# Turning the last batch's queries and keys on TensorE instead of in transposing DMAs

## Chip, cores and metric

The kernel runs on one core of a Trainium2 chip. The metric is device time in microseconds (us); lower is better. Engines are called as the profile calls them: PE (TensorE; PEld is its weight load), DVE (VectorE), ACT (ScalarE), POOL (GpSimd), SP (SyncE, which here only issues transfers).

## What is computed

Chunked attention over q, k, v of shape (4 batches, 8 heads, 768 rows, 64), and on its result x (4, 768, 512) a Fourier mixing and an MLP:

```python
for c in range(nc):                       # chunks of 32 rows
    k_full = concat([mem_k, k[c_start-16 : c_end+8]])    # clipped at the ends; v alike
    a = softmax(q_c @ k_full.T / sqrt(D))
    out[c] = a @ v_full
x = out.transpose(0, 2, 1, 3).reshape(B, S, H * D)
u = x + real(fft(fft(x, axis=1), axis=2))
un = (u - mean(u)) / sqrt(var(u) + 1e-6)
out = u + relu(un @ w_ch1) @ w_ch2
```

## The kernel before

**Stages.** The four batches go through three stages each: attention for 4 pairs of heads (two heads share the 128 partitions), Fourier mixing, MLP. A pair is numbered n = 0 to 15; batch b has the pairs 4b to 4b+3.

*Attention of a pair* (`attention(n)`). POOL loads q and k in bf16 into qs and ks (three buffers each), 8 rows of a head side by side in one partition. Both must be turned, so that the 64 head dimensions lie on the partitions. SP loads v into va (four buffers). PE forms the scores sc of 64 queries against 128 keys in two halves g (`e_scores`, L433 is its matmul), ACT takes the exponential e (L440), PE forms the weighted values xa (L456) and DVE divides by the sums into xsb (L466, L467).

*Two ways of turning.* Batches below `TURNED` (3 before, so batches 0 to 2) turn on PE: `e_turn_q` and `e_turn_k` issue 16 transposes each (L374) into a PSUM tile trq or trk, and ACT copies them to qT (`e_qT`, L391) and to kTb (`e_kT`, L415). From batch 1 on trq and trk share one PSUM bank, "tr". Batch 3 turns by DMA: its loads come as two transfers each, one per head, in pieces of 64 elements (L343; the other batches have one transfer in pieces of 512, L347), then SP issues one transposing transfer for q into qT (`e_flip_q`, L379) and one for k into kU (`e_flip_k`, L382), and ACT copies kU to kTb (L410). The eight rows of a partition then stand apart in qT, so the scores of batch 3 read q and write sc in strides (L430, L431). Two memsets of kU at the start (L851) go with this way.

*Fourier mixing* (`fourier(b)`): folds on DVE and ACT (zy, pq, ff, hi, lo), matmuls with cosine and sine tables into ps (L528, for the first batch L668), split again into up, matmuls over the columns into pm (L679, L579), sums into xsb on DVE. For batches 1 to 3 the lower half of the attention's result goes out to DRAM and comes back in reversed row order: x_rows on POOL (L562), x_back on SP (L566, L567), xr on POOL (L571); it is added at L586 and L588. Statistics (L693) and un on ACT (L699) follow, and for batches 1 to 3 SP turns un into unT by transposing transfers (`e_flip`, L711).

*MLP* (`mlp(b)`): in two halves of 384 rows, 16 groups ph of 4 matmuls (L741), each with a relu on ACT into hT (L749), then 3 groups pc of 16 matmuls (L756), each with a sum on DVE into osb (L763) and a transfer out (L768, or through DRAM for the reversed rows, L771 and L778).

**The order.** Nothing of it is left to a runtime scheduler: class `Plan` simulates the engines ahead of time, with the cost of each task, the transfers' shares and landings (`late` adds to a landing), counts of free buffers (`take` and `give`) and due times, and each engine's instructions are issued in the order that this gives. PE's MLP tasks have the lowest priority and fill the time in which no attention or mixing task of a later batch is ready. `behind` keeps a task from being issued ahead of another: the loads of pair 12 were behind batch 1's xr (`t_xr[b - 2]`) because pair 12 is `TURNED * HP`; other loads are behind the load of the pair before. On the chip each engine works through its own list in order and waits at semaphores.

Of the kernel before, what the change touches and what calls it, by code (L numbers as in the profile page):

```python
# [177 lines left out]
def kernel(  # L178
# [58 lines left out]
    ks = [spool.tile([KP, 2, RB * D], BF16, name=f"ks{i}") for i in range(NS)]  # L237
# [4 lines left out]
    kU = [spool.tile([P, RB, KS], BF16, name=f"kU{i}") for i in range(NKU)]  # L242
    kTb = [spool.tile([P, NT, P], BF16, name=f"kTb{i}") for i in range(NKT)]

    TURNED = 3
    cp_q = "p h j d -> p h (j d)"
    HP = H // 2
    seq = [(b, pr) for b in range(B) for pr in (0, 2, 1, 3)]
# [89 lines left out]
    def e_load_qk(n, i):  # L338
        b, pr = seq[n]
        src, dst = ((q, qs), (k, ks))[i]  # L340
        if b >= TURNED:
            for hh in range(2):
# [65 lines left out]
    def e_kT(n, eng=None):  # L408
        if n >= TURNED * HP:
            nc.scalar.copy(  # L410
# [10 lines left out]
    def e_scores(n, g):  # L421
        qT, kT = qT_of[n], kTb[n % NKT]
        sc_of[n, g] = sc = aps.tile([P, 2, 8, 64], FP32, tag="sc", bufs=1, name="sc")
        for t6 in range(6):
            t = 6 * g + t6
            for hh in range(2):
                r0 = 64 * hh
                if n < TURNED * HP:
                    own, to = qT[r0:r0 + 64, ts(t, 64)], sc[:, hh, t6, :]
                else:  # L430
                    own = strided(qT[r0:r0 + 64], t * 64 // RB, [[QP, RB], [1, 64 // RB]])  # L431
                    to = strided(sc[:, hh, t6, :], 0, [[1, RB], [RB, 64 // RB]])
                nc.tensor.matmul(to, kT[r0:r0 + 64, t, :], own, start=True, stop=True,  # L433
                                 tile_position=(r0, 0))
# [415 lines left out]
    t_gate, LATE, t_flip = None, 1.0, [None]  # L850
    t_uz = add("POOL", 0.4, lambda: [nc.gpsimd.memset(kU[i], 0.0) for i in range(NKU)], rank=20)  # L851

    def attention(n):
        nonlocal t_gate
        b, pr = seq[n]
        first = b == 0
        lq, lk = [add("POOL", 1.6 if b >= TURNED else 0.9, lambda i=i: e_load_qk(n, i),
                      take=(("qs", "ks")[i],), moved=3.1 if b >= TURNED else 1.2, grain=0.032 if b >= TURNED else 0.1, late=LATE if b else 0.0,
                      behind=t_gate if n == HP else t_xr[b - 2] if n == TURNED * HP else t_ck.get(n - 1),
                      rank={0: -4 + i, 1: -1.2 + 0.1 * i, 2: 10 + 0.1 * i}.get(n)) for i in range(2)]  # L860
        lv = add("SP", 2.5, lambda: e_load_v(n), [t_ones[n] if n < NV else None],
                 behind=t_x2.get(b - 2),
                 take=("va",), moved=2.6, grain=0.031, head=0.4, late=(0.0, 4.0, LATE, LATE)[b])
        t_lv[n] = lv
        t_ck[n] = lk
        if n == HP - 1:
            def e_gate():
                nc.gpsimd.tensor_copy(gate[64:65], va[n % NV][64:65, 1, NT - 1, 0:1])

            t_gate = add("POOL", 0.1, e_gate, [lv])  # L870
        mk = t_mk[n] = add("DVE", 0.2, lambda: e_mkT(n), [t_mkT, t_kTz[n % NKT], t_mk.get(n - 1)],
                           take=("kTb",))
        if b >= TURNED:
            eq = add("SP", 1.2, lambda: e_flip_q(n), [lq], take=("qT",), give=("qs",),
                     late=5.0, loose=True, behind=t_flip[0])
            t_flip[0] = tk = add("SP", 1.2, lambda: e_flip_k(n), [lk, t_uz], take=("kU",),
                                 give=("ks",), late=5.0, loose=True, behind=eq)
            ek = add("ACT", 2.05, lambda: e_kT(n), [tk, mk], give=("kU",))
        else:
            tq = add("PE", 0.40, lambda: e_turn_q(n), [lq, t_idb], take=("tr",), give=("qs",))  # L880
            dve = ("DVE", nc.vector.tensor_copy) if n < HP else ("ACT", None)
            eq = add("ACT", 0.80, lambda: e_qT(n), [tq], take=("qT",), give=("tr",),
                     rank=SINES - 0.5 if n == 0 else None)
            ktag = "acc" if first else "tr"
            tk = add("PE", 0.43, lambda: e_turn_k(n), [lk, t_idb, t_kz if n == 0 else t_kzs],
                     take=(ktag,), give=("ks",))
            ek = add(dve[0], 1.25 if dve[1] else 1.04, lambda: e_kT(n, dve[1]), [tk, mk],
                     give=(ktag,))
        for g in range(2):
            s_ = add("PE", 0.32, lambda g=g: e_scores(n, g), [eq, ek], take=("sc",),  # L890
                     give=("qT", "kTb") if g == 1 else ())
            t_sc[n, g] = s_
            t_exp[n, g] = x_ = add("ACT", 1.12, lambda g=g: e_exp(n, g),
                     [s_, t_masks, t_after.get(n)], take=("e1",), give=("sc",))
            tag = "mlp" if first and g == 1 else "xa"
            v_ = add("PE", 0.85, lambda g=g: e_values(n, g), [x_, lv, t_low[n % NV]], take=(tag,),
                     rank=len(plan.tasks) + (50 if (n, g) == (2, 1) else 25) if first else None,
                     give=("e1", "va") if g == 1 else ("e1",))
            take = ("xsb",) if g == 0 and n % HP == 0 else ()
            t_norm[n, g] = add("DVE", 0.78, lambda g=g: e_norm(n, g),  # L900
                               [v_, t_norm[n - n % HP, 0] if (n % HP, g) != (0, 0) else None],
                               take=take,
                               give=(tag,))
        return x_
# [142 lines left out]
    def columns_of(b, t_rest):  # L1047
        t_dn, t_un, cols = {}, {}, {}
        allr = list(t_rest.values())
        kts, sa = (0, 1, 2, 3, 4, 5), None  # L1050
        if b == 0:
            for par in range(2):
                for ab in range(2):
                    t_dn[par, ab] = add("DVE", 0.36, lambda par=par, ab=ab: e_dn(b, par, ab),
                                        [t_rest[par, ab]],
                                        take=("dn",) if (par, ab) == (0, 0) else ())
        else:
            kts = (0, 1, 3, 4, 2, 5)

        def columns(kt):  # L1060
            if b > 0 and kt > 2:
                if kt == 3:
                    cols[kt] = add("PE", 0.7, lambda: e_last_row(b), [t_sum[0]])
                return
            give = (("up",) * 4 if kt == 2 else ("dn",) if kt == 5 else ())
            cols[kt] = add("PE", 0.9, lambda: e_columns(b, kt),
                           allr + [t_rows] + (list(t_dn.values()) if kt > 2 else []),
                           take=("acc",), rank=len(plan.tasks) + (15 if kt == 3 else 0),
                           give=give)

        t_sum = {}
        columns(kts[0])
        for i, kt in enumerate(kts):
            if i + 1 < NST and not (b > 0 and kts[i + 1] == 3):
                columns(kts[i + 1])
            if b == 0 or kt < 3:
                su = add("DVE", 0.7, lambda kt=kt: e_sum(b, kt), [cols[kt]],
                         give=("acc",) if b == 0 else ())
                t_sum[kt] = su
                if b > 0 and kt == 0:  # L1080
                    columns(3)
            else:
                su = add("DVE", 0.8, lambda kt=kt: e_sum_back(b, kt - 3),
                         [cols.get(kt), t_sum[kt - 3], t_xr[b]],
                         give=("acc", "dn") if kt == 5 else ("acc",))
            sa = add("DVE", 0.9, lambda kt=kt: e_stats(b, kt), [su, sa])
            un = add("ACT", 0.72, lambda kt=kt: e_un(b, kt), [sa], take=("un",))
            if b > 0:
                t_un[kt] = add("SP", 1.2, lambda kt=kt: e_flip(b, kt),
                               [un], behind=t_un.get(kts[i - 1]) if i else None,  # L1090
                               take=("unT",) if i == 0 else (), give=("un",), late=2.5,
                               loose=True)
                continue
            tp = add("PE", 0.26, lambda kt=kt: e_turn_u(b, kt), [un, t_idh], take=("mlp",),
                     give=("un",))
            t_un[kt] = add("DVE", 0.43, lambda kt=kt: e_unT(b, kt), [tp, t_un.get(kt - 1)],
                           take=("unT",) if kt == 0 else (), give=("mlp",))
        rs = add("POOL", 1.0, lambda: e_rstd(b), [sa])
        return t_un, rs
# [89 lines left out]
```

## Time and profile before

| | us |
|---|---|
| median of 3 runs (lowest, highest) | 291.2 (290.92, 291.56) |
| the profiled execution | 290.92 |
| its span, first to last instruction | 289.2 |
| PE busy in it | 272.9 (94%) |
| ACT, DVE, POOL busy | 167.7, 166.0, 65.1 |
| mean granted clock of PE | 0.999 |

How to read it: a group of instructions has its line, engine, operation, out<-in with the shape, the count, then busy us and mean ns of one, then the idle time just before them with what ended it. The mean of a PE matmul is the time from its start to its modelled end; matmuls overlap, so a block of several is read from the chain of work or from start to start. In the chain, each piece has its start, its length and what it was. The table of stretches has the busy time of each engine between two times.

### The profile page before, as it was taken

What the parts mean: (1) busy time and instruction counts of PE and PEld (TensorE: products, weight loads), DVE (VectorE), ACT (ScalarE), POOL (GpSimd) and SP (SyncE); (2) the same over time, 40 slices, a digit from 0 to 9 for tenths busy, and PEclk for the clock granted to TensorE, in tenths of its full rate; (3) what the DMA queues carried; (4) which work ended last, traced back from release to release, by engine and by line L of the source; (5) the groups of instructions that cost most, each with busy time, mean ns of one, the idle gap of its engine ahead of it and who ended that gap; (6) DMA issues with size and microseconds to landing.
All of it is one profiled execution on the core that took longest, in us unless ns stands there. A gap on an engine that the chain in (4) does not pass through costs nothing.

```text
span 289.2 us, 7127 instructions
## 1 busy us (share of the span) xinstructions
PE 272.9 (94%) x2932; PEld 170.5 (59%) x2932; DVE 166.0 (57%) x345; ACT 167.7 (58%) x290; POOL 65.1 (23%) x115
## 2 busy tenths in 40 slices
PE   1588989999999999999999999999999999999994
PEld 1466678866665767556676656556654544645641
DVE  7967998862239876958675984985672012012011
ACT  6887446688777587836796466526660721712700
POOL 8844893330210172441001002010020000000000
PEclk9999999999999999999999999999999999999999
DMA  6998989999999999999797047784142504004204
GB/s 110 198 174 150 199 159 206 199 201 195 198 190 257 130 223 166 138 152 220 177 173 176 27 111 145 175 141 159 20 89 85 100 9 125 14 36 105 42 36 109
DMA packets 115968, 39.92 MB, mean 138 GB/s; under 512 B 104544, under 2 KB 111200, under 8 KB 115936
## 3 DMA queue, kind: packets, MB, share of 16 engines
q1 hardware_dynamic: 93744, 23.41, 44.8%
q0 software_dynamic: 21472, 15.21, 32.5%
q10 hardware_dynamic: 720, 0.85, 0.9%
q8 instruction: 23, 0.38, 0.5%
q14 instruction: 9, 0.07, 0.1%
HBM read 37.36 MB, written 13.37 MB: 175 GB/s over the span
## 4 chain that ended last, share of the span: by engine, by line
PE 85%; DVE 6%; POOL 5%; DMA 2%; issue 2%; ACT 0%; POOLq 0%
PE pc L756 29%; PE ph L741 29%; PE xa L456 7%; PE ps L528 5%; PE pm L679 5%; PE sc L433 3%; DMA ks<-in_k_dram 2%; PE trk L374 1%; DVE ff L615 1%; PE trq L374 1%; POOL qs L347 1%; DVE hl L635 1%; DVE up L545 1%; DVE xsb L467 1%; PE pm L579 1%
## 5 line engine op out<-in xcount | busy, mean ns | idle before, releaser
L749 ACT ACTIVATE hT<-ph 128x384 f16<-128x384 f32 x128 | 61.9, 491 | 50.6 <-PE ph L741 49.8
L741 PE MATMUL ph<-unT,w_sb 128*128 128x384 f16 x512 | 88.1, 326 | 0.0
L756 PE MATMUL pc<-w_sb,hT 128*128 128x512 f16 x384 | 87.8, 380 | 0.0
L741 PEld LDWEIGHTS <-w_sb 128*128 128x128 f16 x512 | 48.6, 98 | 32.0 <-issue 0.4
L756 PEld LDWEIGHTS <-hT 128*128 128x128 f16 x384 | 35.9, 98 | 41.0 <-issue 0.4
L763 DVE SCALAR_TENSOR_TENSOR osb<-pc,rstd,xsb 128x512 f32<-128x512 f32 x24 | 18.0, 751 | 69.3 <-PE pc L756 64.8
L440 ACT ACTIVATE e<-sc,mbias 128x384 f32<-128x384 f32 x64 | 33.6, 577 | 18.8 <-PE sc L433 18.8
L456 PEld LDWEIGHTS xa<-va,e 128*64 128x64 f32 x672 | 21.9, 137 | 7.2 <-issue 6.2
L456 PE MATMUL xa<-va,e 128*64 128x65 f32 x672 | 25.8, 226 | 0.0
L699 ACT ACTIVATE un<-xsb,mu_s 128x512 f16<-128x512 f32 x24 | 16.9, 719 | 6.6 <-DVE mu_s L694 6.6
L540 ACT CAST up<-ps 128x386 f16<-128x386 f32 x16 | 9.6, 602 | 13.8 <-PE ps L528 11.6
L693 DVE BATCH_NORM_STATS2 st<-xsb 128x6 f32<-128x512 f32 x24 | 16.6, 691 | 0.7
L467 DVE TENSOR_TENSOR xsb<-xa,zs 128x384 f32<-128x384 f32 x28 | 15.6, 558 | 1.0
L466 DVE RECIPROCAL zs<-xa 128x6 f32<-128x6 f32 x28 | 5.3, 190 | 18.1 <-PE xa L456 17.7
L518 DVE TENSOR_TENSOR lo<-ff,hi 128x768 f16<-128x768 f32 x12 | 11.4, 954 | 4.7 <-ACT hi L513 4.7
L545 DVE TENSOR_TENSOR up<-ps,up 128x386 f16<-128x386 f32 x16 | 9.5, 596 | 6.9 <-ACT up L540 6.7
L433 PE MATMUL sc<-qT,kTb 64*128 64x64 bf16 x384 | 12.6, 205 | 0.5 <-ACT e L440 0.5
L433 PEld LDWEIGHTS <-kTb 64*128 64x128 bf16 x384 | 8.5, 100 | 7.3 <-issue 6.1
L571 POOL DMA_DIRECT2D xr<-x_back x3 | 2.3, 778 | 44.3 <-DMA x_back<-x_rows 44.3
L513 ACT CAST hi<-ff 128x768 f16<-128x768 f32 x12 | 9.9, 827 | 3.3 <-DVE ff L505 3.0
L374 PE MATMUL trq<-ident_b,qs 96*64 96x96 bf16 x192 | 7.0, 220 | 5.1 <-DMA qs<-in_q_dram 5.1
L685 DVE TENSOR_TENSOR xsb<-pm,xsb 128x512 f32<-128x512 f32 x15 | 10.0, 672 | 3.2 <-PE pm L679 3.2
(150 smaller groups left out, 356.9 us busy)
## 6 DMA issues: line engine op xcount, KB each, us to landing
va<-in_v_dram SPq DMA_DIRECT2D x32, 220.0 KB
w_sb<-in_moe_w_ch_dram POOLq DMA_DIRECT2D x8, 512.0 KB, 15.1
out_dram<-osb SPq DMA_DIRECT2D x12, 256.0 KB
qs<-in_q_dram POOLq DMA_DIRECT2D x12, 192.0 KB, 6.2
ks<-in_k_dram POOLq DMA_DIRECT2D x12, 192.0 KB, 6.9
x_rows<-xsb POOLq DMA_DIRECT2D x3, 768.0 KB, 5.1
xr<-x_back POOLq DMA_DIRECT2D x3, 768.0 KB, 6.5
out_rows<-osb SPq DMA_DIRECT2D x9, 256.0 KB
```

Source lines behind the costliest of these rows:

```text
L433: nc.tensor.matmul(to, kT[r0:r0 + 64, t, :], own, start=True, stop=True, tile_position=(r0, 0))
L440: nc.scalar.activation(e1[:, :, :, ts(half, 32)], sc[:, :, 0:6, ts(half, 32)], AFT.Exp, bias=mbias[:, half:half + 1], scale=1.0 / math.sqr ...
L456: nc.tensor.matmul(xa[64 * half:64 * half + 64, st, hh, 0:65], e1[:, hh, t6, :], v1[:, hh, 6 * g + t6, 0:65], start=True, stop=True)
L467: nc.vector.tensor_tensor(xs[b][:, 3 * g:3 * g + 3, 2 * pr * D:(2 * pr + 2) * D] .rearrange("p s (h d) -> p s h d", h=2), xa[:, :, :, 0:D] ...
L528: nc.tensor.matmul(out_[:, sp, :], part[:, ab, sp * 3 + st, c0:c1], tab[:, sp, st, :], start=(st == 0 and i == 0), stop=(st == 2 and i == 1))
L679: nc.tensor.matmul(pm[:, par, :], lhs, rhs[:, par, :], start=(im == 0), stop=(im == 3))
L693: nc.vector.bn_stats(st6, xs[b][:, kt, :])
L699: nc.scalar.activation(un, xs[b][:, kt, :], AFT.Identity, bias=mu_of[b][:, kt, 0:1], scale=-1.0)
L741: nc.tensor.matmul(ph[:, 0:384], w1_sb[:, dt, ts(ht, P)], unT_of[b][:, dt, sh * 384:(sh + 1) * 384], start=(dt == 0), stop=(dt == NDT - 1))
L749: nc.scalar.activation(hT_of[b, sh][:, ht, :], ph[:, 0:384], AFT.Relu, bias=0.0, scale=-1.0)
L756: nc.tensor.matmul(pc_of[b, sh, stl], hT_of[b, sh][:, ht, ts(stl, P)], w2_sb[:, ht, :], start=(ht == 0), stop=(ht == NHT - 1))
L763: nc.vector.scalar_tensor_tensor(osb, pc, rstd_of[b][:, st:st + 1], xs[b][:, st, :], ALU.mult, ALU.add)
```

## The change

`TURNED` goes from 3 to 9. There are four batches, so every batch now turns q and k on PE: for pairs 12 to 15 the plan adds the two turns on PE, and the copy of q on ACT reads PSUM; the 8 transposing transfers and the 16 loads by head fall away, 8 loads of the common kind take their place, and the copy of k reads trk instead of kU. The hold of pair 12's loads behind batch 1's xr no longer applies (no pair is number 36), so they come behind pair 11's. The memsets of kU stay in the program.

In `e_scores` two lines are ordered differently, with the same meaning. In the plan, the time that a transposing transfer is given to land after its issue goes from 5.0 to 1.6 for q and k (no longer reached) and from 2.5 to 1.6 for unT.

```diff
-    TURNED = 3
+    TURNED = 9
...
-                if n < TURNED * HP:
-                    own, to = qT[r0:r0 + 64, ts(t, 64)], sc[:, hh, t6, :]
-                else:
+                own, to = qT[r0:r0 + 64, ts(t, 64)], sc[:, hh, t6, :]
+                if n >= TURNED * HP:
                     own = strided(qT[r0:r0 + 64], t * 64 // RB, [[QP, RB], [1, 64 // RB]])
                     to = strided(sc[:, hh, t6, :], 0, [[1, RB], [RB, 64 // RB]])
...
             eq = add("SP", 1.2, lambda: e_flip_q(n), [lq], take=("qT",), give=("qs",),
-                     late=5.0, loose=True, behind=t_flip[0])
+                     late=1.6, loose=True, behind=t_flip[0])
             t_flip[0] = tk = add("SP", 1.2, lambda: e_flip_k(n), [lk, t_uz], take=("kU",),
-                                 give=("ks",), late=5.0, loose=True, behind=eq)
+                                 give=("ks",), late=1.6, loose=True, behind=eq)
...
                 t_un[kt] = add("SP", 1.2, lambda kt=kt: e_flip(b, kt),
                                [un], behind=t_un.get(kts[i - 1]) if i else None,
-                               take=("unT",) if i == 0 else (), give=("un",), late=2.5,
+                               take=("unT",) if i == 0 else (), give=("un",), late=1.6,
                                loose=True)
```

The changed kernel has one line less from L428 on: L433 becomes L432, L741 becomes L740 and so on.

## Prediction

> **What bounds the kernel now.** I read the page's slices first, then the busy time by stretch, then the chain of work that ended last.
>
> ```profile
> PE   1588989999999999999999999999999999999994
> ...
> PEclk9999999999999999999999999999999999999999
> ...
> PE 85%; DVE 6%; POOL 5%; DMA 2%; issue 2%; ACT 0%; POOLq 0%
> ```
>
> From the seventh slice on PE is busy nine tenths or more, at the full granted clock, and 85% of the chain lies on it. A digit 9 may still hide small gaps, so I asked for the busy time of each engine in five stretches (columns: stretch, its length, then PE, PEld, DVE, ACT, POOL busy, clock, DMA share, GB/s):
>
> ```profile
> 47.00:118.60 71.60, 71.48 (x1048) 48.14 (x1046) 46.95 (x98) 53.00 (x93) 19.49 (x28) 1.00 1.24 192
> 118.60:170.60 52.00, 52.00 (x583) 32.14 (x583) 37.64 (x76) 35.03 (x56) 6.65 (x9) 1.00 0.94 153
> 170.60:212.60 42.00, 42.00 (x316) 26.32 (x315) 30.83 (x56) 23.83 (x45) 3.20 (x4) 1.00 0.57 123
> 212.60:285.20 72.60, 72.60 (x384) 37.37 (x382) 9.87 (x16) 25.47 (x52) 1.59 (x2) 1.00 0.28 68
> ```
>
> PE is busy 238.08 of the 238.2 us from 47.0 to 285.2, and the view of waits for that stretch names none on PE. MLP matmuls of earlier batches fill every hole that attention and mixing leave. So from 47 us on the kernel's time is the sum of PE's work; what other engines and queues do counts only if it makes PE wait. The last 4.0 us (285.2 to 289.2) are the last osb and its transfer, and 1.7 us lie outside the span (290.92 against 289.2).
>
> The order of instructions of both programs tells where they part. On PE they are the same up to 118.6 us of this trace; ACT, DVE and SP part at about the same place, POOL at 80 us. The start is therefore the same, with its two memsets of kU, which stay although nothing reads kU any more. The last 64 ph and 48 pc matmuls, the osb and the transfer are the same too. The price is made between 118.6 and 212.6 us.
>
> **Part 1: PE's added and removed work.** The prices are in the chain, in order of time (columns: start, us, what):
>
> ```profile
> 110.12 0.46 PE trq L374 x16
> ...
> 115.71 0.47 PE trk L374 x16
> ...
> 118.68 0.28 PE sc L433 x12
> ...
> 131.71 0.44 PE sc L433 x12
> ...
> 274.85 10.37 PE pc L756 x48
> 285.25 0.75 DVE osb L763
> ```
>
> Added: batch 3 has 4 head pairs, and each now gets a trq block and a trk block of 16 transposes. They cost 0.46 and 0.47 us where PE is saturated, so 4 x (0.46 + 0.47) = 3.72 us. I take the blocks, not the mean of 220 ns of one transpose: that is latency, and the starts lie some 29 ns apart. Removed: the scores of batch 3 read q in strides and write in strides. Their 8 blocks (131.7 to 168 us) take 0.44 us each, while those of batches 1 and 2 take 0.28; the batch now has the short form. That is 8 x 0.16 = 1.28 us back. Nothing else on PE changes in number: 512 ph, 384 pc, 301 ps, 138 pm, 384 sc and 768 value matmuls stand in both programs. A change from a small tile (sc, xa, trq, trk) to a large one costs about 0.1 us (eight pc take 1.83 us ahead of a small tile and 1.73 ahead of a large one); there are 47 such changes before and 47 after, so I add nothing for them. Sum: 3.72 - 1.28 = +2.44 us, all on the path, since PE has no gap to put it in.
>
> One rule speaks much louder against the change. The trace's row is 0.46 us for 16 transposes at a granted clock of 1.00. The Trainium skill ("TensorE: Matmul & The Clock Gate", Part 4: PE-mode transpose) has about 275 ns for one bf16 transpose within a kernel, because the access latency dominates, and says that transposes don't count as busy for the clock gate. By 275 ns, 128 transposes would cost 35.2 us and the kernel would end at about 325 us; by the row it is 3.72 us, and the measured blocks decide.
>
> **Part 2: the other engines.** The four rows that change on ACT:
>
> ```profile
> L391 ACT COPY qT<-trq 128x768 bf16<-128x768 bf16 x12 | 9.6, 797 | 3.0 <-PE trq L374 3.0
> ...
> L415 ACT COPY kTb<-trk 128x1056 bf16<-128x1056 bf16 x8 | 8.3, 1038 | 0.6 <-PE trk L374 0.6
> L410 ACT COPY kTb<-kU 128x1056 bf16<-128x1056 bf16 x4 | 8.2, 2059 | 1.5 <-DMA kU<-ks 1.5
> ```
>
> ACT gains 4 qT copies of 0.80 and its 4 kTb copies go from 2.06 to 1.04: 3.2 - 4.1 = -0.9 us, on an engine that is busy 59 of the 94 us. No gain in time: PE did not wait for it.
>
> POOL issues 8 loads at 0.64 us in place of 16 at 0.77 us (5.1 against 12.3). The loads of pair 12 now go ahead of batch 1's x_rows, those of pair 13 ahead of its xr. Pair 12's k load needs trk of pair 9, done at 86.1 us; x_rows was issued at 86.56 and now goes at about 86.8, with 192 KB ahead of it. Its x_back and xr follow; xr was issued at 100.31, lands some 6.5 us later and is first read at 116.37, so nearly 10 us cover it. rstd of batch 1 now stands behind pair 15's k load (issued at about 122.9) and runs at 123.6, against 123.75 before.
>
> SP loses 8 transposes of some 1.25 us, which stood between the v loads, the six unT transposes of batch 1 and x_back of batch 2. All of those go earlier or stay. PE waited for none of them, so I count nothing.
>
> **Part 3: the shorter landing in the plan** (1.6 for 2.5 us) only moves unT's use in PE's order. Batch 3's unT transposes were issued from 207.5 to 216.3 us and their first reader stands at 243.7; batch 2's were done at 177.7, with their reader at 197.7. Nothing, with 20 us and more of cover.
>
> **Part 4: new waits.** What before does not show is how PE waits in the new order. Below zero it can't go, since PE waits nowhere after 47 us. From above I walked the new PE order with the block times of the chain, from 118.9 us: trq and trk of pair 12 stand at 118.9 and 122.4, of 13 at 126.7 and 129.3, of 14 at 132.6 and 134.1, of 15 at 136.7 and 148.2. Two things can be late.
>
> The loads: those of pair 14 are issued at 110.5 and 116.1, of 15 at 119.4 and 122.9 (each needs the buffer that the transposes of three pairs earlier leave). The same instruction before:
>
> ```profile
> DMA to landing us min/median/max: 4.1/6.5/19.0
> ```
>
> With 6.5 us the least cover (119.4 to 136.7, 17.3 us) leaves 10.8; with the worst, 19.0, q of pair 15 comes 1.7 us late. The strided loads in this very stretch landed in at most 8.9, so I take zero and keep 1.7.
>
> The one tr bank: trq, its copy to qT, trk, its copy to kTb, and the next trq wait for each other. By ACT's order trk of pair 14 comes 0.3 us after qT's copy ends, trq of pair 15 0.4 us after kTb's, the others 0.7 us and more. If one pair of exps (1.05 us) came ahead of the copy at both tight spots, PE would lose 2 x 1.05 - 0.7 = 1.4 us. The same ring served batches 1 and 2 with no wait of PE after 47 us, so I take zero and keep 1.4.
>
> **Sum.** 290.92 + 2.44 = 293.4 us against the profiled execution. The median of the runs lies 0.28 above that execution; I forecast 293.5.
>
> **Rivals.** *PE waits in the new order*: both prices of part 4, up to +3.1 more, so 294 to 296.6. For it: margins of 0.3 and 0.4 us, and a denser attention stage (four pairs between 119 and 164). Against it: no wait in the same pattern of batches 1 and 2. 10%.
>
> *Not slower, by transposes that fit beside matmuls*: if their weight loads and drains overlapped with the neighbours, a block would cost less than it shows. The point from which this decides is 1.28 / 8 = 0.16 us a block; at 0.13 the time would be 290.92 + 1.04 - 1.28 = 290.7. Against it: the blocks' 0.46 is already from start to start between neighbours, with no gap. 6%.
>
> *Removed transfers were slowing PE*: the 8 transposes and 768-packet loads gone, DMA's share falls (0.94 in the stretch 118.6 to 170.6). But 48 pc take 10.36 us with DMA idle or busy, and 20 take 4.42 in both 121 and 192 us. It would give about 292, hardly less. 4%.
>
> **Numbers.** My forecast, with waits under 0.5 us in sum: 80% (293.0 to 294.1). What a measurement can tell from no change is about 0.2%, 0.6 us. The first rival is slower as well, the third mostly; the second splits between same and faster. So slower 0.91, same 0.05, faster 0.04. The range reaches a little into the third case and over half of the first: 292.6 to 295.2.
>
> **What would show it.** Right: trq and trk blocks of 0.46 and 0.47 between 118 and 150 us, sc blocks of 0.28 throughout, PE busy about 275.3 us (272.9 + 2.44), still no waits of PE after 47 us, the last pc at about 287.7. Wrong: waits of PE on ACT's qT or kTb copy, or on ks or qs; transpose blocks much off 0.46; or a start before 118 us that is not the same.

## The result and the profile after

The changed kernel took 293.76 us (median of 5 runs, 293.64 to 294.54) against 291.13 us of the kernel before (5 runs): ratio 1.0094, 95% interval 1.0078 to 1.0109. It is slower, by 2.6 us or 0.9%. The profiled execution took 293.64 us, with a span of 291.9.

The slices of the page and the chain's shares, of the changed kernel:

```profile
PE   1588989999999999999999999999999999999994
...
PEclk9999999999999999999999999999999999999999
...
PE 86%; POOL 5%; DVE 4%; DMA 2%; issue 1%; POOLq 0%
```

The stretches (columns as before; the last two borders lie later, since the program is longer):

```profile
47.00:118.60 71.60, 71.60 (x1060) 48.42 (x1061) 46.90 (x98) 53.11 (x93) 14.91 (x22) 1.00 1.09 194
118.60:170.60 52.00, 52.00 (x703) 33.49 (x702) 38.88 (x79) 35.53 (x61) 4.50 (x6) 1.00 0.61 118
170.60:215.00 44.40, 44.40 (x328) 27.28 (x325) 31.50 (x58) 23.56 (x46) 4.80 (x6) 1.00 0.59 129
215.00:287.80 72.80, 72.80 (x385) 37.45 (x383) 8.26 (x11) 24.33 (x50) 0.00 (x0) 1.00 0.26 64
```

PE is busy in every microsecond from 47.0 to 287.8, 275.1 us in all for 272.9 before, and waits for nothing. DMA's share between 118.6 and 170.6 fell from 0.94 to 0.61 and the time rose: the queues were not the bound.

The chain of the changed kernel where the new blocks stand:

```profile
119.28 0.46 PE trq L374 x16
...
122.83 0.47 PE trk L374 x16
...
132.96 0.46 PE trq L374 x16
133.42 0.71 PE xa L455 x24
134.13 0.28 PE sc L432 x12
134.41 0.49 PE trk L374 x16
...
137.02 0.46 PE trq L374 x16
...
148.38 0.36 PE trk L374 x16
...
277.44 10.37 PE pc L755 x48
287.84 0.75 DVE osb L762
```

Seven of the eight blocks (two of them left out here) cost 0.46 to 0.49 us, the last 0.36; the scores cost 0.28.

**A ruler for the rest.** The start of the kernel, which is the same in nearly all of these programs, drifts by up to 1.3 us from one profiled execution to the next, as its first loads land (the chain of work has 5.32 us for one k load before and 6.11 for the same load after). So I measure from the first transpose of pair 9's k, at about 86 us, to the start of the last 48 pc matmuls, which every kernel with at least ten pairs turned on PE has in common: PE works without a gap between them unless it waits. The first of these transposes, before and after, on the timeline:

```profile
85.64 0.55 PE L374 MATMUL trk<-turn_b,ks 100*64 100x100 bf16 x16
```

```profile
85.96 0.55 PE L374 MATMUL trk<-turn_b,ks 100*64 100x100 bf16 x16
```

Before: 85.64 to 274.85, 189.21 us. After: 85.96 to 277.44, 191.48 us. The change cost PE 2.27 us; 0.32 of the two profiled executions' difference is the start.

### The profile page after: what moved, and what is told of

It is laid out like the page before. It is cut to its first block, busy times and chain, and to the rows that moved or that the text cites. A ratio compares the mean times of both kernels' runs of the same rounds, so it can differ in the third digit from the quotient of the medians.

```text
span 291.9 us, 7361 instructions
## 1 busy us (share of the span) xinstructions
PE 275.1 (94%) x3060; PEld 172.8 (59%) x3060; DVE 166.8 (57%) x345; ACT 166.5 (57%) x294; POOL 57.6 (20%) x107
## 4 chain that ended last, share of the span: by engine, by line
PE 86%; POOL 5%; DVE 4%; DMA 2%; issue 1%; POOLq 0%
PE ph L740 29%; PE pc L755 29%; PE xa L455 7%; PE ps L527 5%; PE pm L678 5%; PE sc L432 3%; DMA ks<-in_k_dram 2%; PE trk L374 2%; PE ps L667 2%; PE trq L374 2%; DVE ff L614 1%; POOL qs L347 1%; DVE hl L634 1%; DVE xsb L466 1%; PE pm L578 1%
## 5 line engine op out<-in xcount | busy, mean ns | idle before, releaser
L740 PE MATMUL ph<-unT,w_sb 128*128 128x384 f16 x512 | 87.9, 326 | 0.0
L740 PEld LDWEIGHTS <-w_sb 128*128 128x128 f16 x512 | 48.6, 98 | 32.4 <-issue 0.6
L391 ACT COPY qT<-trq 128x768 bf16<-128x768 bf16 x16 | 12.7, 797 | 4.9 <-PE trq L374 4.9
L347 POOL DMA_DIRECT2D qs<-in_q_dram x16 | 10.5, 658 | 24.1 <-PE trq L374 14.9
L374 PE MATMUL trq<-ident_b,qs 96*64 96x96 bf16 x256 | 9.1, 218 | 6.4 <-DMA qs<-in_q_dram 6.4
L347 POOL DMA_DIRECT2D ks<-in_k_dram x16 | 10.3, 644 | 23.3 <-PE trk L374 22.8
L415 ACT COPY kTb<-trk 128x1056 bf16<-128x1056 bf16 x12 | 12.5, 1040 | 0.7 <-PE trk L374 0.6
```

The lines of the kernel that those rows point to most:

```text
L347: nc.gpsimd.dma_start(dst[n % NS][0:QP], src[b, 2 * pr:2 * pr + 2].rearrange("h (p j) d -> p h (j d)", j=RB))
L374: nc.tensor.transpose(out_[64 * hh:64 * hh + 64, j * w:(j + 1) * w], src[:, hh, j * D:(j + 1) * D], eye)
L740: nc.tensor.matmul(ph[:, 0:384], w1_sb[:, dt, ts(ht, P)], unT_of[b][:, dt, sh * 384:(sh + 1) * 384], start=(dt == 0), stop=(dt == NDT - 1))
```

## Experiments

"Ruler" is that length in the profiled execution; the times are medians, compared with runs of the kernel before on the same chip.

| kernel | median us | before | ratio (95%) | ruler us |
|---|---|---|---|---|
| after | 293.76 | 291.13 | 1.0094 (1.0078, 1.0109) | 191.48 |
| shorter landings only | 292.62 | 291.36 | 1.0038 (1.0018, 1.0058) | 190.74 |
| batch 3 turned twice | 296.58 | 291.36 | 1.0170 (1.0141, 1.0199) | 194.26 |
| strided scores kept | 294.76 | 291.36 | 1.0105 (1.0076, 1.0134) | 192.74 |
| batches 2, 3 by DMA | 330.12 | 291.36 | 1.1318 (1.1272, 1.1364) | - |
| the same, pair 12 held | 317.93 | 290.96 | 1.0937 (1.0914, 1.0960) | - |
| pairs 14, 15 by DMA | 292.65 | 290.96 | 1.0056 (1.0043, 1.0068) | 190.39 |
| pairs 10 to 15 by DMA | 296.52 | 290.96 | 1.0153 (1.0120, 1.0187) | 197.00 |
| after without kU memsets | 293.80 | 290.96 | 1.0104 (1.0084, 1.0125) | 191.48 |
| pairs 10 to 15, x_back first | 294.71 | 291.35 | 1.0088 (1.0055, 1.0120) | 189.88 |
| pairs 11 to 15, x_back first | 290.74 | 291.35 | 0.9982 (0.9968, 0.9997) | 188.88 |
| strided reading only | 289.87 (1 run) | 291.35 | - | 187.93 |
| strided writing only | 291.33 (1 run) | 291.35 | - | 189.21 |

### Is the price PE's work? Transposes twice, and the strides put back

Each transpose block of batch 3 twice:

```diff
-        turn(trq, qs[n % NS], ident_b[0:QP, 0:QP])
+        for _ in range(2 if n >= 3 * HP else 1):
+            turn(trq, qs[n % NS], ident_b[0:QP, 0:QP])
```

and trk likewise.

> The changed kernel with each transpose block of batch 3 issued twice in a row into the same bank, in the same order otherwise. Theory: each extra block costs its 0.46 to 0.47 us on PE, 4 x 0.93 = +3.7 us over the changed kernel, 297.4 us. Rival (transposes fit beside the neighbouring matmuls and cost under 0.16 us a block): under 295.1 us.

The ruler grew by 2.78 us over the changed kernel, not 3.7. The chain of this kernel:

```profile
119.91 0.80 PE trq L374 x32
...
123.80 0.83 PE trk L374 x32
...
151.43 0.71 PE trk L374 x32
```

Two blocks in a row take 0.80 and 0.83, so the second costs 0.34 to 0.36 us. The rival is out (it needed under 0.16), and the theory's 0.46 is mended: 0.34 to 0.36 is the 16 transposes, and some 0.12 comes once with a block. Beside an xa that 0.12 is mostly not paid a second time: the trk after an xa takes 0.36 above and 0.71 doubled here, twice the bare block, and the xa after a trq took 0.71 instead of 0.85. Beside an sc it is paid in full (0.28 and then 0.49 above). In the rows the transposes and xa have shapes of 64 columns (96\*64, 100\*64, 128\*64), sc has 64\*128. So I read the 0.12 as the price of a change of shape, but no run tests that.

The strided form of the scores, put back on queries turned by PE:

```diff
-                if n >= TURNED * HP:
+                if n >= 3 * HP:
                     own = strided(qT[r0:r0 + 64], t * 64 // RB, [[QP, RB], [1, 64 // RB]])
...
+        if n >= 3 * HP:
+            nc.scalar.copy(qT, tr_of.pop(n))
+            return
```

> The changed kernel, but q of batch 3 is copied straight out of PSUM, so that its rows stand apart as the DMA left them, and the scores of batch 3 read and write in strides. Theory: the 0.44 us blocks come back, 8 x 0.16 = +1.28 us over the changed kernel, 295.0 us. Rival (the long blocks of before came from q's arrival by DMA or from the transfers beside them, not from the strides): blocks of 0.28 us and 293.8 us.

The first of the eight blocks in its chain:

```profile
126.52 0.44 PE sc L435 x12
```

All eight are 0.44 again and the ruler grew by 1.26 us (1.28 expected), with the transfers of the changed kernel. So the price belongs to the strides, not to q's arrival by DMA.

### Half of the change

Pairs 14 and 15 by DMA, 12 and 13 on PE: the conditions on `TURNED` become conditions on the pair, and as in the changed kernel nothing holds pair 12's loads.

```diff
-    TURNED = 3
+    FLIP = 14
...
-        if b >= TURNED:
+        if n >= FLIP:
```

> Pairs 14 and 15 turned by DMA, 12 and 13 on PE: half of the change. Theory (price by pair on PE; the trace of the changed kernel gave 2.27 us for four pairs): 1.1 us under the changed kernel, 292.5 us, PE without waits after 47 us. Rival (the change's price was one of order, not of PE's work): near one of the two ends, 291.2 or 293.7 us, or PE waits.

The ruler is 1.18 us above before and 1.09 below after: half, as the price by pair has it. PE waits for nothing.

### The shorter landings alone

> Batch 3 still turned by DMA; only the planned landings of the transposing transfers are cut to 1.6 us. Theory (PE is saturated after 47 us and time is the sum of its work): PE's work is the same, so 291.1 us as before, within 0.5, and no PE wait after 47 us. Rival (the plan relied on the long landings: with 1.6 instead of 5.0 PE meets scores or ph whose operand has not landed): PE waits on qT or kTb of batch 3, 292 to 294 us.

The edit is the three `late` lines of the change, with `TURNED` at 3. The rival was right: 1.3 us slower by the medians, 1.1 by the ratio. PE's waits in this kernel after 45 us (line, who released it, us in total, times, longest):

```profile
PE sc L433 <- ACT e L440: 1.0, 1, 1.0
PE sc L433 <- ACT kTb L410: 0.5, 1, 0.5
```

1.5 us of waits, and the ruler is 1.53 longer. Only 0.5 of it is on kTb directly; the exps of the other wait stood on ACT behind a kTb copy that had waited 2.5 us for kU. Here, where q and k of batch 3 are turned by DMA, the plan that believed in early landings put scores too early into PE's order. It is the landings of q and k that do it: with `TURNED` at 3, the line for unT alone leaves the program of before unchanged, and the two lines for q and k alone give the program measured here. In the changed kernel all three lines do nothing: built with the old landings and `TURNED` at 9, it has the same instructions with the same waits in the same order on every engine. So the whole price of the change is that of `TURNED`.

### The other way: more pairs by DMA

If PE's work is the bound, turning batch 2 by DMA as well should gain as much as the change lost.

```diff
-    TURNED = 3
+    TURNED = 2
...
-                      behind=t_gate if n == HP else t_xr[b - 2] if n == TURNED * HP else t_ck.get(n - 1),
+                      behind=t_gate if n == HP else t_ck.get(n - 1),
```

> The kernel before with batch 2 turned by DMA as well (its loads go behind the pair before). Theory in its pure form: PE loses another 3.72 us of transposes and gains 1.28 us of strided scores, -2.4 us, 288.7 us, as long as PE waits nowhere. Rival (loads by head and transposing transfers of batch 2 meet the busiest time of the transfer queues, DMA share above 1 from 47 to 118 us, and PE runs out of attention and mixing work to fill or waits on qT and kTb): 291 us or more, with PE waits on ACT's kTb or on qT.

It took 330 us. PE's waits in its profiled execution (324.63 us, the shortest of eight), the two longest in total:

```profile
PE sc L433 <- ACT e L440: 11.7, 4, 8.1
PE sc L433 <- ACT kTb L410: 11.4, 2, 8.6
```

xr of batch 1 was issued at 140.6 us, behind loads on POOL that waited for transposing transfers. I suspected that order, and put the hold of pair 12 back:

> As the kernel with batches 2 and 3 turned by DMA (330 us), but pair 12's loads are again held behind batch 1's xr, as in the kernel before. Theory A (that kernel lost because xr of batch 1 stood on POOL behind loads that waited for the transposing transfers, so that batch 1's MLP, PE's filling work, came late): xr of batch 1 is issued by 115 us instead of 140.6, and the time falls below 300 us. Theory B (the transposing transfers themselves land up to 10 us late among x_back and the v loads, and the scores wait for kTb whatever the order): over 310 us, with PE waits on kTb.

xr went out at 121.5 us, and the time fell by 12 us, to 317.9. That is neither below 300 (theory A) nor a sign that the order did not matter; PE still waited 9.7 us on kTb, 7.0 on unT and 5.1 on hT. Theory B has its time and its wait on kTb, but since xr did not go out by 115 us, theory A's condition was not met, and how the loss divides between the two stays open. With two pairs more instead of four:

> Pairs 10 to 15 turned by DMA, two more than in the kernel before, with pair 12's loads held behind batch 1's xr as before. Theory (price by pair, as long as the transfers arrive): 1.1 us under the kernel before, 290.0 us. Rival (the two pairs fall into the stretch in which the transfer queues are full, DMA share 1.2 to 2.2 from 101 to 123 us): PE waits for kTb and 292 us or more.

296.5 us, the rival's side, though the wait was on unT and not on kTb. PE's longest wait in its trace (an execution of 298.87 us, above that kernel's median), and the chain there:

```profile
PE ph L741 <- DMA unT<-un: 5.6, 1, 5.6
```

```profile
127.08 0.59 DVE xsb L586
127.97 1.44 SPq L711
129.50 1.31 SPq L711
130.90 4.30 DMA unT<-un
135.29 1.44 PE ph L741 x4
```

PE ran out of everything: attention and mixing were done up to there, and batch 1's MLP waited for unT. xr was first added (DVE L586) at 120.2 us instead of 116.4, and x_back had gone out on SP at 102.2 us instead of 91.6, behind the transposing transfers of pairs 10 and 11:

```profile
91.63 0.57 SPq L566 DMA_DIRECT2D x_back<-x_rows  x1
```

```profile
100.83 1.31 SPq L382 DMA_TRANSPOSE kU<-ks  x1
102.23 0.61 SPq L566 DMA_DIRECT2D x_back<-x_rows  x1
```

The first line is of before, the others of this kernel. I took that for the cause. The trace does not prove it: xr had landed by 116.6, so DVE came to it late by its own order, and SP issued v loads from 119.5 to 127.3, between unT's first transpose (118.1) and the next (128.0). Nor is the stop likely to be all of it: two of the six executions kept a mean granted clock of 1.00, where this one had 0.988 (see the last section), and still took 293.59 and 295.25 us. As a test I put x_back ahead of the transposing transfers:

```diff
             eq = add("SP", 1.2, lambda: e_flip_q(n), [lq], take=("qT",), give=("qs",),
-                     late=5.0, loose=True, behind=t_flip[0])
+                     late=5.0, loose=True, behind=t_flip[0] or t_x2[1])
```

> Pairs 10 to 15 turned by DMA, as in the kernel that took 296.5 us, but SP issues x_back of batch 1 ahead of the transposing transfers of pairs 10 and 11. Theory (that kernel lost because x_back went out at 102.2 us instead of 91.6, so that xr, unT and the MLP of batch 1 came late and PE stood still for 5.6 us at 130 us): no PE wait on unT, and the price by pair holds, 290.0 us, under both kernels. Rival (the transposing transfers of the two pairs are late wherever they stand, since the queues are full there): PE waits again, on kTb or unT, 292 us or more.

> The same with pairs 11 to 15 turned by DMA, one more than in the kernel before. Theory: 0.57 us under the kernel before, 290.5 us, no PE wait. Rival: 292 us or more.

With five pairs by DMA PE waits 0.2 us in all, and the kernel is the fastest here of those that compute the whole reference: 290.74 us, ratio 0.9982 (0.9968 to 0.9997) to before. The ruler is 0.33 us shorter than before, of 0.57 expected, and 2.60 shorter than after. The added line has no share in that: with four pairs by DMA it leaves the program of before unchanged. With six pairs x_back went out at 94.4 us and the long stop is gone from the profiled execution (291.28 us, one of the fastest): two waits remain, 0.8 us on unT and 1.1 on xsb. But nine of that kernel's twelve runs took 293.9 to 295.7 us, and its median of 294.71 is on the rival's side. What those nine waited for was not recorded. Their mean granted clock was 0.988 to 0.994, against 0.997 to 0.999 in the other three, which would fit a long stop of PE in them (see the last section); that part stays open.

### The dead memsets

> The changed kernel without the two memsets of kU, which nothing reads there. Theory (they stand on POOL at 15 to 17 us, in the chain ahead of the loads of pair 2, and PE starts its saturated stretch later by what they take): 1 to 1.9 us under the changed kernel, 292.2 us. Rival (the loads' landing of 5 to 6 us is set by the transfers beside them, or another wait takes over): 293.7 us.

293.8 us, and the ruler, which begins after the start, is that of the changed kernel (191.48); in this execution it begins at 87.27 us, later than in any other. No gain. Chain of this kernel, then of the changed one, at the start:

```profile
8.65 8.45 DMA ks<-in_k_dram
```

```profile
15.95 1.11 POOL kU L850
...
17.65 6.11 DMA ks<-in_k_dram
```

In the changed kernel a chain of POOL work, the memsets among it, led to the load of pair 2. Without them, the chain goes through an earlier load that takes 8.45 us. The transfers of the start are late either way; which of the rival's two reasons holds, the runs do not separate.

### Whose price are the strides?

The kernel before, with the strides on one side only; first its writing, then its reading put in order:

```diff
-                    to = strided(sc[:, hh, t6, :], 0, [[1, RB], [RB, 64 // RB]])
+                    to = strided(sc[:, hh, t6, :], 0, [[64 // RB, RB], [1, 64 // RB]])
```

```diff
-                    own = strided(qT[r0:r0 + 64], t * 64 // RB, [[QP, RB], [1, 64 // RB]])
+                    own = strided(qT[r0:r0 + 64], t * 64, [[64 // RB, RB], [1, 64 // RB]])
```

> The kernel before, but the scores of batch 3 read q in strides (elements 192 bytes apart) and write sc in order; so the queries of a tile of batch 3 stand in another order in the output. If the long blocks come from the reading: 0.44 us a block. If from the writing: 0.28 us. No theory of the change hangs on it; it says whose price the 1.28 us is.

> The kernel before, but the scores of batch 3 read q in order (so they take other queries than the tile's, and the output of batch 3 is of other queries) and write sc in strides of 32 bytes. If the long blocks come from the writing: 0.44 us a block. If from the reading: 0.28 us.

(The reading is in runs of 8 elements, 16 bytes, whose starts are 192 bytes apart; the expectation says elements.) A block of batch 3 on the timeline, strided reading only, then strided writing only:

```profile
131.87 0.35 PE L433 MATMUL sc<-qT,kTb 64*128 64x64 bf16 x12
132.15 2.12 PE L741 MATMUL ph<-unT,w_sb 128*128 128x384 f16 x12
```

```profile
132.06 0.51 PE L433 MATMUL sc<-qT,kTb 64*128 64x64 bf16 x12
132.50 2.12 PE L741 MATMUL ph<-unT,w_sb 128*128 128x384 f16 x12
```

From start to start 0.28 and 0.44 us, as in all eight blocks of each. Reading in runs is free here; writing PSUM in elements 32 bytes apart costs all of it, and the ruler of the first is 1.28 us shorter than before, of the second equal.

## Why the prediction was right

**The bound.** Forecast: time is the sum of PE's work after 47 us. The doubled blocks, the strides put back and the half change moved the ruler by 2.78, 1.26 and 1.18 us, with no wait in any of them. The bound holds as long as work arrives; in the kernels with six and eight pairs turned by DMA it no longer does.

**Part 1.** +2.44 forecast, 2.27 measured. Removed: 1.28 forecast, 1.26 by experiment. Added: 3.72 forecast; the eight blocks sum to 3.63, and the xa after one of them took 0.71 in place of 0.85, which makes about 3.5. Mis-sized was the price of a block: I put 0.46 or 0.47 for all eight, but two stood beside an xa, where 0.11 and 0.14 us less was paid. The count of changes to a large tile, which I put at nothing, was right: from 118.6 us on there are 17 in each chain. The 275 ns for one transpose of the Trainium skill ("TensorE: Matmul & The Clock Gate", Part 4: PE-mode transpose) does not hold as a price in a stream: 16 took 0.34 us. Nor did the transposes cost clock: among matmuls, in blocks of at most 0.49 us and doubled of at most 0.85, the granted clock stayed 1.00 from 118.6 to 170.6 us; a longer stretch of them was not run.

**Part 2.** No gain came from ACT's, POOL's and SP's relief. x_rows went out at 87.43 us (forecast 86.8, and 0.3 later with the start), xr at 104.1, and the first reader still ran at 116.69 (116.37 before). rstd ran at 124.53, 0.6 us later than forecast when the start's 0.32 is counted out; no engine waited for it.

**Part 3.** Nothing, as forecast, but for another reason: the line for unT moved no use of unT; it changes no instruction, neither with `TURNED` at 9 nor at 3. What the shorter landings cost with `TURNED` at 3 came from q's and k's, which the changed kernel no longer reaches.

**Part 4.** The eight blocks came 0.2 to 0.4 us later than the walk through PE's order put them, 0.32 of it the start, and no load made PE wait. The two tight spots held: qT of pair 14 was ready at 134.31 for a trk at 134.41, kTb at 136.50 for a trq at 137.02. These lines are ACT's, of the changed kernel:

```profile
133.51 0.80 ACT L391 COPY qT<-trq 128x768 bf16<-128x768 bf16 x1 [1.74 <-PE trq L374]
...
135.46 1.04 ACT L415 COPY kTb<-trk 128x1056 bf16<-128x1056 bf16 x1
```

The margin was 0.1 us once, so the first rival was near. What a later copy would have cost, no run shows.

**Sum.** 293.5 forecast, 293.76 measured. (The forecast's own terms, 290.92 + 2.44 + 0.28, make 293.6; it was rounded down on the way.) PE was busy 275.1 us, 275.3 forecast. The mechanism is right, but that the sum comes so near is in part luck: PE's part was 0.17 too large, and the two profiled executions differ by 0.32 us before the change begins, with the same instructions there; the forecast had nothing for that.

## What to carry to other kernels

Where one engine is busy without a gap, price an edit by that engine's own work, block by block from start to start and beside the neighbours it will have, and ask of the rest only whether it makes that engine wait. Moving work off such an engine pays as long as the new path delivers in time: here five pairs turned by transfers gained, six and eight lost. One thing to watch is what else stands on the same queue: x_back went out 10 us later and more behind the added transfers, and putting it first brought six pairs from 296.5 to 294.7 us (ratios 1.0153 and 1.0088), still above before. Before comparing traces for a few tenths, choose two events that all of them share; the start alone drifted by up to 1.3 us.

## What was unexpected of the hardware

*A stop of PE costs twice.* In the kernel with six pairs by DMA PE stood for 5.55 us. The stretches around it:

```profile
129.80:135.30 5.50, 0.01 (x1) 0.04 (x2) 0.82 (x2) 0.00 (x0) 0.66 (x1) 0.81 1.41 184
135.30:137.30 2.00, 2.00 (x16) 1.03 (x18) 0.00 (x0) 0.49 (x1) 0.00 (x0) 0.50 0.83 157
137.30:139.30 2.00, 2.00 (x22) 1.32 (x19) 0.95 (x3) 0.00 (x0) 0.00 (x0) 0.50 0.15 35
139.30:141.30 2.00, 2.00 (x12) 1.09 (x10) 1.97 (x3) 1.07 (x3) 1.93 (x3) 0.83 0.97 197
```

The granted clock is 0.50 for 4 us after the stop; four ph take 1.44 us there and 0.65 elsewhere. In finer stretches:

```profile
132.00:133.00 1.00, 0.00 (x0) 0.00 (x0) 0.00 (x0) 0.00 (x0) 0.00 (x0) 1.00 1.11 107
133.00:133.50 0.50, 0.00 (x0) 0.00 (x0) 0.00 (x0) 0.00 (x0) 0.00 (x0) 0.67 0.27 47
133.50:134.00 0.50, 0.00 (x0) 0.00 (x0) 0.00 (x0) 0.00 (x0) 0.00 (x0) 0.50 1.41 229
```

PE's last matmul ended at 129.74, so the clock fell some 3.4 us into the stop. The Trainium skill ("TensorE: Matmul & The Clock Gate", Why this matters for your kernels) says that a gap of more than some 3 us brings the clock to half; this trace agrees.

*Writes into PSUM 32 bytes apart cost, reads in runs of 16 bytes do not* (0.44 and 0.28 us a block, above). The Trainium skill ("PSUM — Partial Sum Buffer", Specifications) has 8-byte lines there and warns of any pattern that is not contiguous; the runs agree for this write. That leaves one thing to try that was not tried here: to read q with single elements in order of rows and write sc in order, which would keep the output right; whether such a reading is as free as one in runs, no run shows.
